# Two token tables instead of four, filled by long rows, and router logits with the router weights stationary in four column groups

## The chip, the cores and the metric

The kernel runs on one core of one Trainium2 chip. The metric is device time in microseconds (us) of one execution, the median of several runs. TensorE (PE) does matmuls, VectorE (DVE) and ScalarE (ACT) the elementwise work, GpSimd (POOL) small elementwise work and the indirect DMAs, and SyncE (SP) issues nearly all other DMAs, in program order.

## The reference, cut to what matters

```python
def _attn_ref(q, k, v, p):                      # batch 8, heads 8, seq 576, head_dim 64, 32 packed rows
    p_packed = sm_attn(p, k, v)
    return sm_attn(q, p_packed, p_packed)

def _moe_ref(x, w_in, w_out):                   # x: 4608 tokens x 512; d_ff 2048
    h = x @ w_in
    return (h * (1.0 / (1.0 + np.exp(-h)))) @ w_out

def _moe2_ref(x, w_gate, w_output_gate, w1, w2):    # 8 experts, F 1024
    logits = x @ w_gate
    e_idx = np.argmax(logits, axis=1)
    probs = softmax(logits)
    gate_w = probs[np.arange(N), e_idx]
    eom = 1.0 / (1.0 + np.exp(-(x @ w_output_gate)))
    for e in range(E):
        mask = e_idx == e
        h = np.maximum(x[mask] @ w1[e], 0.0)
        out[mask] = gate_w[mask, None] * eom[mask, e, None] * (h @ w2[e])
```

w_in and w_out arrive as 64-bit floats.

## The kernel before, in words

**Order.** The order of all instructions on each engine is written out by hand. Eight batches of 576 tokens go through attention and the dense layer. A batch is 16 steps, f = 0 to 15, one for each 128 columns of d_ff. A step (`batch`) runs: `mm1` (first matmul of column block f into the PSUM tile `h`, one buffer), `act` (tanh on ACT, L673, and the product `g` on DVE, L674, which reads `h`), the extra steps listed for position (f, 0), the splits of `g` into a rounded high part (`ghi`, ACT, L679) and a low part (`glo`, DVE, L684), in two of three steps of batches 1 to 6 a slot that splits a piece of expert weights (`shi` on ACT, L483, and a subtraction on DVE, L484), `mm2` for the column block two steps back, and the extra steps of position (f, 1). The next `mm1` needs the tile `h` to be free again. The extra steps at (f, 0) and (f, 1) are the attention of the next batch (s1 to s9: s3 is L579, s5 is L535 with the DVE transposes L603), `step_m` (L535 as ps_m), and the routing of the batch before.

**Batch 0.** It also converts w_in and w_out from 64 bits. `f64_load` brings a piece of 512 KB into one of six buffers, and `f64_conv` turns it into 32 bits by three DVE operations (L452, L455, L458), into `w_in` or into a tile `wf` (pool `stg`, two buffers) that ACT and POOL then split (L469, L470). Two pieces are converted in a step, and each conversion issues the load of the next piece. Value tiles of the next batch come by `load_att`: `v1` of batch 1 is issued at the end of step 5, when s3 of the first half has read the same buffer, and is read by s3 of the second half at the end of step 7.

**Token tables.** Four tables in DRAM (`perm`, 289 x 128 rows of 16 integers, 2.37 MB each) hold the tokens sorted by expert. At the end of step 4 of batch 0 `setup_late` fills them, one with 4608 and three with 0, from a tile of 289 integers per partition: L175, 16 rows of 1156 bytes per partition and table. The fill tiles are two `wf` buffers. Then a zero row of `xr` is written from a tile of its own. Later `place` computes where each token goes, and one indirect DMA for each block of 128 tokens (L782) writes it to table (block number) mod 4. Whoever reads a place (`fetch_ix`, L910) reads all four tables and adds the four (L911, L912).

**Router logits.** After the second matmul of a batch, `row_t` transposes a pair of token blocks (ACT and DVE copy them to SBUF), at steps 3 and 7 of the next batch, and `row_logits` multiplies them with the router weights at (5, 0) and (9, 0): for each of the two blocks 4 matmuls (L265) with the 128 x 128 block stationary and 8 router columns moving. DVE copies the 8 logits of each block out (L269), and when a group of blocks is complete `finish` (L738 to L741) finds the expert of each token. Groups of four blocks complete with the pair at step 9 (in batches 1, 3, 5, 7), groups of five with a single block at step 13 (batches 2, 4, 6). There are 16 pairs, 14 of them inside batches and 2 in `last_rows`, and 4 single blocks.

**Experts.** From about 870 us on, 38 blocks of sorted tokens are gathered and multiplied with their expert's weights.

Of the kernel before, what the change touches and what calls it, by code (L numbers as in the profile page):

```python
# [8 lines left out]
F32 = mybir.dt.float32  # L9
# [3 lines left out]
I32 = mybir.dt.int32  # L13
ALU = mybir.AluOpType
# [10 lines left out]
E8 = 8  # L25
F2 = 1024
NTOK = B * S
NBLK = NTOK // 128
CAP = NBLK
NPAIR = NBLK + E8 - 1  # L30
XW = DM + 1
SCALE = 1.0 / 8.0

C_ID, C_E, C_OFF, C_LT, C_J, C_END = 0, 128, 136, 144, 208, 209
HS = S // 2
EARLY = 3
NSTATIC = NBLK + 2
NPERM = 4
PW = 16


def constants():
    p = np.arange(128)
    c = np.zeros((128, C_END), np.float32)
    c[:, C_ID:C_ID + 128] = np.eye(128)
    e = np.arange(E8)
    c[:, C_E:C_E + E8] = e
    c[:, C_OFF:C_OFF + E8] = (e - E8) * CAP
    c[:, C_LT:C_LT + E8 * E8] = (e[None, :] < e[:, None]).reshape(1, -1)
    c[:, C_J] = p  # L50
    k = np.full((128, 256), 0x3F80, np.uint16)
    k[:, :128] *= p[:, None] < p[None, :]
    t = np.stack([block_tokens(i) for i in range(NBLK)], axis=1).astype(np.int32)
    t[:, np.arange(NBLK) % NPERM > 0] -= NTOK
    t = np.concatenate([t, np.zeros((128, PW - 1), np.int32)], axis=1)
    return {"cst": c, "cstk": k, "cstt": t}

# [24 lines left out]
class Kernel:  # L82
# [12 lines left out]
    def run(self):  # L95
        tc, nc = self.tc, self.nc
        c_const, cp = self.pool("const")
        c_rt, self.rt = self.pool("rt")
        c_p1, self.p1 = self.pool("p1")
        c_in, self.pin = self.pool("pin", "right")  # L100
        c_att, self.pa = self.pool("pa", "right")
        psums = [self.pool(n, space=PSUM) for n in ("ps_acc", "ps_h", "ps_a")]
        self.ps_acc, self.ps_h, self.ps_a = [p for _, p in psums]
        p1 = self.p1

        self.cst = cp.tile([128, C_END], F32, name="cst")
        self.ident = self.cst[:, C_ID:C_ID + 128]
        self.iota8 = self.cst[:, C_E:C_E + E8]
        self.tri = cp.tile([128, 2, 128], BF16, name="tri")
        self.nt_run = cp.tile([128, E8], F32, name="nt_run")  # L110
        self.pick_f = cp.tile([128, 40], F32, name="pick_f")
        self.before = cp.tile([128, E8, E8], F32, name="before")
        self.tb = cp.tile([128, 8, E8], F32, name="tb")
        self.pick_i = cp.tile([128, 8], U32, name="pick_i")
        self.ptab = cp.tile([1, 1 + EARLY], I32, name="ptab")
        self.tab = cp.tile([1, 4, NPAIR], I32, name="tab")

        self.flip = False
        self.ppt, self.m, self.g, self.loads = {}, {}, {}, {}
        self.graws = []  # L120
        self.wgt = cp.tile([128, 4, E8], F32, name="wgt")
        self.tok = self.rt.tile([128, NBLK + PW - 1], I32, name="tok")
        self.w_in = self.pin.tile([128, 4, FF], F32, name="w_in")
        self.a1 = [self.pa.tile([128, 5, 128], F32, name="a1t")]
        self.pp = self.pa.tile([128, 128], F32, name="pp")
        self.a2 = [[p1.tile([128, 2, S], F32R, tag=f"a2_0{i}", name="a2") for i in range(2)], None]
        self.zero = self.rt.tile([128, 512], BF16, tag="junk", bufs=1, name="zero")
        nc.gpsimd.memset(self.zero, 0.0)
        nc.gpsimd.memset(self.a1[0][64:128, 4, :], 0.0)

        self.split_jobs = [(w, e, k) for e in range(E8) for w in (1, 2) for k in range(4)]
        self.split_n, self.split_raw, self.split_loaded, self.split_done = 0, [], [], []
        self.late, self.group = [], None
        self.ch, self.ex, self.x, self.xt, self.hs, self.ht, self.sc = {}, {}, {}, {}, {}, {}, {}

        c_stg, self.stg = self.pool("stg", "right")
        self.wo = self.p2 = self.mid = None
        self.prologue()
        self.batch(0)
        c_stg.close()  # L140
        c_stg, self.stg = self.pool("spl", "right")
        for b in range(1, B - 1):
            self.batch(b)
        while self.split_jobs or self.split_loaded or self.split_done:
            self.split_store()
            self.split_slot()
        c_stg.close()
        c_att.close()
        self.pick()
        self.batch(B - 1, hook=lambda f: self.open_first(f, c_in))  # L150
        self.last_rows()
        c_p1.close()
        c_p2, self.p2 = self.pool("p2")
        c_q2, wp = self.pool("q2")
        self.r2 = tc.queue_regs(depth=2, engines=[ENG.SP, ENG.PE], name="r2")
        self.q2 = wp.queue([128, 4, 2, 2 * DM], F32R, regs=self.r2, name="q2", contiguous=True)
        self.experts()
        for c in (c_q2, c_p2, self.c_q1, *[c for c, _ in reversed(psums)], c_rt, c_const):
            c.close()
# [6 lines left out]
    def setup_late(self):  # L166
        nc = self.nc
        nc.sync.dma_start(self.tri, self.i["cstk"].bitcast(BF16).rearrange("p (a b) -> p a b", a=2))
        nc.sync.dma_start(self.tok, self.i["cstt"])
        nc.gpsimd.memset(self.nt_run, 0.0)  # L170
        for i, perm in enumerate(self.perm):
            if i < 2:
                fill = self.stg.tile([128, E8 * CAP + 1], I32, tag="wf", bufs=2, name="fill")
                nc.gpsimd.memset(fill, 0 if i else NTOK)
            nc.sync.dma_start(perm.rearrange("(p c) w -> p (c w)", p=128).rearrange("p (w c) -> p w c", w=PW),  # L175
                              fill.unsqueeze(1).to_broadcast([128, PW, E8 * CAP + 1]))
        z = self.rt.tile([128, 5, XW], F32, tag="xr", name="zrow")[:1, 0]
        nc.gpsimd.memset(z, 0.0)
        nc.sync.dma_start(self.xr[NTOK:NTOK + 1, :], z)

    def pick(self):
        assert self.group is None and not self.late
# [39 lines left out]
    def last_rows(self):  # L222
# [3 lines left out]
        g = self.rows_group(b, range(4))  # L226
        for j in (3, 0, 1, 2):
            self.mm2_block(self.acc[j], hi[:, j * 128:j * 128 + 128], lo[:, j * 128:j * 128 + 128], NF - 1, False, True)
        for j in (3, 0, 1, 2):
            self.evac(g, j, self.acc[j])  # L230
        acc = self.ps_acc.tile([128, 512], F32, tag="acc3", name="accL")
        side = {2: lambda: self.row_t(g, 3, 0), 5: lambda: self.row_logits(g, 3, 0),
                6: lambda: self.row_t(g, 1, 2), 9: lambda: self.row_logits(g, 1, 2),
                12: lambda: self.place(g)}
        for ff in range(NF):
            self.mm2_block(acc, self.gl[0][:, ff, :], self.gl[1][:, ff, :], ff, ff == 0, ff == NF - 1)
# [22 lines left out]
            g["t"][j] = t  # L259

    def row_logits(self, g, *js):
        ps = self.ps_a.tile([128, 2, 512], F32, tag="a", name="ps_rl")
        for n, j in enumerate(js):
            for k in range(4):
                self.nc.tensor.matmul(ps[:, 0, n * E8:n * E8 + E8], g["t"][j][:, k * 128:k * 128 + 128], self.wgt[:, k, :],  # L265
                                      start=(k == 0), stop=(k == 3))
        for n, j in enumerate(js):
            g["left"] -= 1
            self.nc.vector.tensor_copy(out=g["lg"][:, g["at"][j], :], in_=ps[:, 0, n * E8:n * E8 + E8])  # L269
        if not g["left"]:  # L270
            self.finish(g)

# [64 lines left out]
    def batch(self, b, hook=None):  # L337
        sched = self.extra_steps(b)
        for f in range(NF):
# [34 lines left out]
                    self.f64_load(t[:, i], True)  # L374
            if b == 0 and f == 14:
                self.mid = self.rt.tile([128, E8 * DM], F32, tag="wg", name="mid")
                self.nc.sync.dma_start(self.wgt, self.i["wgt"])
            if b == 0 and f == 15:
                self.split_load()
                self.split_load()  # L380
# [5 lines left out]
    def extra_steps(self, b):  # L386
        sched = {}

        def at(f, pos, fn):
            sched.setdefault((f, pos), []).append(fn)  # L390
# [13 lines left out]
        if b > 0:  # L404
            js = [(3, 0), (1, 2)] + ([(4,)] if b % 2 == 0 else [])
            for n, r in enumerate(js):
                at(4 * n + 3, 0, lambda r=r: self.row_t(self.group, *r))
                at(4 * n + 5, 0, lambda r=r: self.row_logits(self.group, *r))
            at(4 * len(js) + 3, 0, lambda: self.place(self.group))
        for c in range(1, 8):  # L410
            at(2 * c - 2 + (b == 0 and (c == 1 or c % 2 == 0)), 0, lambda c=c: self.step_m(b, c))
# [487 lines left out]
    def fetch_ix(self, j):  # L899
        nc = self.nc  # L900
# [3 lines left out]
        else:  # L904
            off = nc.values_load(self.tab[0:1, 0, j:j + 1], engines=[ENG.SP], min_val=0, max_val=E8 * CAP * 128)
            self.ex[j] = nc.values_load(self.tab[0:1, 1, j:j + 1], engines=[ENG.SP], min_val=0, max_val=E8 - 1)
        ix = self.rt.tile([128, NPERM + 2], I32, tag="xix_p", bufs=4, name="xix_p")
        at = self.rt.tile([128, 1], I32, tag="xix", bufs=6, name="xix")
        for i, perm in enumerate(self.perm):
            nc.sync.dma_start(ix[:, i:i + 1], perm[bass.ds(off, 128), 0:1])  # L910
        nc.gpsimd.tensor_tensor(out=ix[:, 4:6], in0=ix[:, 0:2], in1=ix[:, 2:4], op=ALU.add)  # L911
        nc.gpsimd.tensor_tensor(out=at, in0=ix[:, 4:5], in1=ix[:, 5:6], op=ALU.add)  # L912
        return at.bitcast(U32)

    def flag(self, j):
# [134 lines left out]
```

## Time and profile before

| what | value |
|---|---|
| median of 3 runs | 1361.1 us (1360.93 to 1362.29) |
| profiled execution | 1360.51 us, span 1358.7 us from first to last instruction |
| TensorE | busy 1269.3 us (93%), mean granted clock 0.971 |
| VectorE | 653.9 us (48%) |
| ScalarE | 505.8 us (37%) |
| GpSimd | 173.4 us (13%) |
| DMA | 247.72 MB, 182 GB/s on average |

Busy shares are averages over the whole span; the stages differ. A row of the timeline gives the start, the busy time, the engine and line, the operation, and in brackets how long the engine sat idle before it and what ended that.

### The profile page before, as it was taken

The numbers are of one execution on the slowest core, as the hardware profiler recorded it, in microseconds if no ns is written. First come the engines' busy times: TensorE is split into PE (matmuls) and PEld (weight loads), VectorE is DVE, ScalarE is ACT, GpSimd is POOL, SyncE is SP. The second block draws the span as 40 slices with busy tenths as digits, with TensorE's granted clock in tenths as the row PEclk, the third lists the DMA queues.
The fourth block names the chain that finished last, engine by engine and source line by source line (L and its number), as shares of the span: only waits on it lengthen the run. The fifth ranks groups of instructions, "written<-read, shape, count | busy, mean of one in ns | idle before, by whom it ended". The sixth has DMA issues, their size and how long they took to land. (4 is left out here: it accounts for less than half of the span.)

```text
span 1358.7 us, 24463 instructions
## 1 busy us (share of the span) xinstructions
PE 1269.3 (93%) x8414; PEld 1020.1 (75%) x8416; DVE 653.9 (48%) x1417; ACT 505.8 (37%) x980; POOL 173.4 (13%) x236
## 2 busy tenths in 40 slices
PE   7754699999999899999999999999999999999997
PEld 3543578778788688787787788878888888888886
DVE  6953965845865745857556745232222222222221
ACT  3321255445464444454454433223223222222322
POOL 0220310100010100101000111112212212211210
PEclk9686899999999999999999999999999999999999
DMA  7598346846695855776665414442557383722630
GB/s 292 205 233 210 110 151 222 274 158 223 211 292 180 257 197 189 227 285 209 225 219 193 104 32 157 108 127 71 193 173 249 121 301 97 277 66 69 236 129 23
DMA packets 118303, 247.72 MB, mean 182 GB/s; under 512 B 30177, under 2 KB 56609, under 8 KB 118178
## 3 DMA queue, kind: packets, MB, share of 16 engines
q1 hardware_dynamic: 110946, 226.35, 51.0%
q0 software_dynamic: 7232, 19.72, 4.4%
q8 instruction: 77, 1.26, 0.4%
q14 instruction: 48, 0.39, 0.1%
HBM read 401.92 MB, written 96.29 MB: 367 GB/s over the span
## 5 line engine op out<-in xcount | busy, mean ns | idle before, releaser
L715 PE MATMUL acc<-wo,ghi 128*128 128x512 f32 x1024 | 320.9, 395 | 0.0
L715 PEld LDWEIGHTS acc<-wo,ghi 128*128 128x128 f32 x1024 | 194.5, 190 | 39.0
L664 PE MATMUL ps_h<-a,m_hi 128*128 128x288 f32 x1024 | 215.5, 303 | 0.8 <-DVE a L630 0.8
L715 PE MATMUL acc<-wo,glo 128*128 128x512 f32 x512 | 212.9, 416 | 0.0
L664 PE MATMUL ps_h<-a,m_lo 128*128 128x288 f32 x512 | 163.5, 319 | 30.9 <-DVE g L674 25.2
L1007 PE MATMUL py<-queue_q_buf,hhi 128*128 x608 | 190.7, 395 | 0.0
L979 PE MATMUL pu<-queue_q_buf,xhi 128*128 x560 | 174.6, 393 | 0.0
L664 PEld LDWEIGHTS ps_h<-a,m_hi 128*128 128x128 f32 x1024 | 171.1, 196 | 2.7 <-DVE a L630 1.0
L993 DVE TENSOR_TENSOR hlo<-ph,hhi 128x512 fp32r<-128x512 f32 x76 | 49.0, 686 | 247.3 <-ACT hhi L992 247.3
L674 DVE SCALAR_TENSOR_TENSOR g<-g,ps_h 128x576 f32<-128x576 f32 x128 | 96.1, 751 | 131.0 <-ACT g L673 130.2
L673 ACT ACTIVATE g<-ps_h 128x576 f32<-128x576 f32 x128 | 83.3, 651 | 188.8 <-PE ps_h L664 186.0
L664 PEld LDWEIGHTS ps_h<-a,m_lo 128*128 128x128 f32 x512 | 99.8, 195 | 57.0 <-DVE g L674 33.3
L1007 PEld LDWEIGHTS py<-queue_q_buf,hhi 128*128 128x128 f32 x608 | 114.5, 188 | 25.6
L715 PEld LDWEIGHTS acc<-wo,glo 128*128 128x128 f32 x512 | 97.3, 190 | 43.0 <-issue 24.8
L1007 PE MATMUL py<-queue_q_buf,hlo 128*128 x304 | 122.9, 404 | 0.0
L979 PEld LDWEIGHTS pu<-queue_q_buf,xhi 128*128 128x128 f32 x560 | 105.3, 188 | 22.4
L782 POOL DMA_INDIRECT perm<-tok,dsti x36 | 38.9, 1081 | 647.9 <-DVE dsti L779 507.4
L679 ACT CAST ghi<-g 128x512 fp32r<-128x512 f32 x128 | 79.4, 620 | 107.6 <-DVE g L674 106.5
L979 PE MATMUL pu<-queue_q_buf,xlo 128*128 x280 | 113.7, 406 | 0.3 <-ACT hs L981 0.3
L981 ACT ACTIVATE hs<-pu 128x512 f32<-128x512 f32 x76 | 45.4, 598 | 164.2 <-PE pu L979 162.5
L684 DVE TENSOR_TENSOR glo<-g,ghi 128x512 fp32r<-128x512 f32 x128 | 88.5, 692 | 31.1 <-ACT ghi L679 26.2
L1012 POOL DMA_INDIRECT out<-y,xix x38 | 38.2, 1006 | 328.2 <-ACT y L1010 320.6
(183 smaller groups left out, 1501.1 us busy)
## 6 DMA issues: line engine op xcount, KB each, us to landing
queue_q_buf<-ws SPq DMA_DIRECT2D x70, 4096.0 KB
ws<-shi SPq DMA_DIRECT2D x64, 512.0 KB
mid<-in_w SPq DMA_DIRECT2D x48, 512.0 KB
ws<-mid SPq DMA_DIRECT2D x48, 512.0 KB
att_v<-in_v SPq DMA_DIRECT2D x15, 640.0 KB
perm<-fill SPq DMA_DIRECT2D x4, 2312.0 KB
og<-in_wog SPq DMA_DIRECT2D x35, 256.0 KB
att_k<-in_k SPq DMA_DIRECT2D x15, 576.0 KB
```

Of the source, the lines that this page charges most:

```text
L664: nc.tensor.matmul(ps[:, hf, :288], lw[:, qd, fs], rx[:, qd, ts], start=(i == 0), stop=(i == 5))
L673: nc.scalar.activation(out=g2, in_=ps[:, :, :288], func=AF.Tanh, scale=0.5)
L674: nc.vector.scalar_tensor_tensor(out=g2, in0=g2, scalar=1.0, in1=ps[:, :, :288], op0=ALU.add, op1=ALU.mult)
L679: self.nc.scalar.copy(out=hi, in_=self.graw[:, :512])
L684: self.nc.vector.tensor_tensor(out=lo, in0=self.graw[:, :512], in1=self.ghi.bitcast(F32), op=ALU.subtract)
L715: self.nc.tensor.matmul(acc, l, r, start=(first and i == 0), stop=(last and i == 2))
L782: nc.gpsimd.indirect_dma_start(out=self.perm[(i0 + r) % NPERM], out_offset=bass.IndirectOffsetOnAxis(ap=di[:, r:r + 1], axis=0), in_=self. ...
L979: nc.tensor.matmul(ps, l[:, ks], w[:, k, r, ns], start=(i == 0), stop=(i == 11))
L981: nc.scalar.activation(out=self.hs[j][:, n * 512:n * 512 + 512], in_=ps, func=AF.Relu)
L993: nc.vector.tensor_tensor(out=lo[:, n], in0=ps, in1=hi[:, n].bitcast(F32), op=ALU.subtract)
L1007: nc.tensor.matmul(ps, l[:, k // 4, ks], w[:, k // 2, r, (k % 2) * DM:(k % 2) * DM + DM], start=(i == 0), stop=(i == 23))
L1012: nc.gpsimd.indirect_dma_start(out=self.out, out_offset=bass.IndirectOffsetOnAxis(ap=ix[:, 0:1], axis=0), in_=y, in_offset=None, bounds_ch ...
```

## The change

The four tables become two. Both are filled with half of 4608 (and the token numbers are shifted by as much), from one tile of 2312 integers per partition, in two rows of 9248 bytes per partition and table; the tile lies in the `xr` buffer, not in the `wf` buffers. The zero row comes from a tile that is zero already. A place is read from two tables, with one addition. Blocks go to table (block number) mod 2.

For a pair of token blocks the logits now take 8 matmuls with 32 columns of router weights stationary (8 of the quarter meant, the rest of other quarters or zero) and 128 token columns moving, in four column groups of 32: two halves of the contraction for each of the two blocks. ACT copies the 128 x 128 result into SBUF, over the first 128 columns of the transposed second block, and after `mm2` of the same step, at (f, 1) and ahead of the attention's step there, one matmul with that copy stationary and a 0/1 selection of 16 columns moving adds the halves and turns the result back. It writes 16 columns of the tile `h` behind the columns that `act` has read. The copies of the logits and `finish` follow there. In `last_rows` the first part moves from block 5 to 4 and from 9 to 8, and the second takes its place. Single blocks stay as they were.

```diff
-C_ID, C_E, C_OFF, C_LT, C_J, C_END = 0, 128, 136, 144, 208, 209
+C_ID, C_E, C_OFF, C_LT, C_J, C_SEL, C_END = 0, 128, 136, 144, 208, 209, 225
-NPERM = 4
+NPERM = 2
...
+    n = np.arange(2 * E8)
+    c[:, C_SEL:] = (p[:, None] % 32 == n % E8) & (p[:, None] // 32 % 2 == n // E8)
...
-    t[:, np.arange(NBLK) % NPERM > 0] -= NTOK
+    t -= NTOK // NPERM
...
-        self.wgt = cp.tile([128, 4, E8], F32, name="wgt")
+        self.wgt = cp.tile([128, 3 * E8 + 32], F32, name="wgt")
...
-        for i, perm in enumerate(self.perm):
-            if i < 2:
-                fill = self.stg.tile([128, E8 * CAP + 1], I32, tag="wf", bufs=2, name="fill")
-                nc.gpsimd.memset(fill, 0 if i else NTOK)
-            nc.sync.dma_start(perm.rearrange("(p c) w -> p (c w)", p=128).rearrange("p (w c) -> p w c", w=PW),
-                              fill.unsqueeze(1).to_broadcast([128, PW, E8 * CAP + 1]))
-        z = self.rt.tile([128, 5, XW], F32, tag="xr", name="zrow")[:1, 0]
-        nc.gpsimd.memset(z, 0.0)
-        nc.sync.dma_start(self.xr[NTOK:NTOK + 1, :], z)
+        n = (E8 * CAP + 1) * PW // 2
+        fill = self.rt.tile([128, 5 * XW], I32, tag="xr", name="fill")[:, :n]
+        nc.gpsimd.memset(fill, NTOK // NPERM)
+        for perm in self.perm:
+            nc.sync.dma_start(perm.rearrange("(p c) w -> p (c w)", p=128).rearrange("p (h n) -> p h n", h=2),
+                              fill.unsqueeze(1).to_broadcast([128, 2, n]))
+        nc.sync.dma_start(self.xr[NTOK:NTOK + 1, :].rearrange("o (p c) -> (o p) c", p=3), self.zero.bitcast(F32)[:3, :XW // 3])
...
-        side = {2: lambda: self.row_t(g, 3, 0), 5: lambda: self.row_logits(g, 3, 0),
-                6: lambda: self.row_t(g, 1, 2), 9: lambda: self.row_logits(g, 1, 2),
+        side = {2: lambda: self.row_t(g, 3, 0), 4: lambda: self.row_logits(g, 3, 0), 5: lambda: self.row_logits2(g, (3, 0)),
+                6: lambda: self.row_t(g, 1, 2), 8: lambda: self.row_logits(g, 1, 2), 9: lambda: self.row_logits2(g, (1, 2)),
                 12: lambda: self.place(g)}
...
     def row_logits(self, g, *js):
+        nc = self.nc
         ps = self.ps_a.tile([128, 2, 512], F32, tag="a", name="ps_rl")
-        for n, j in enumerate(js):
+        if len(js) == 1:
             for k in range(4):
-                self.nc.tensor.matmul(ps[:, 0, n * E8:n * E8 + E8], g["t"][j][:, k * 128:k * 128 + 128], self.wgt[:, k, :],
-                                      start=(k == 0), stop=(k == 3))
+                nc.tensor.matmul(ps[:, 0, :E8], g["t"][js[0]][:, k * 128:k * 128 + 128], self.wgt[:, k * E8:k * E8 + E8], start=(k == 0), stop=(k == 3))
+            self.row_logits_out(g, ps[:, 0, :E8], js)
+            return
+        for k in (0, 2, 1, 3):
+            for n, j in enumerate(js):
+                c = 2 * (k // 2) + n
+                nc.tensor.matmul(ps[32 * c:32 * c + 32, 0, :128], self.wgt[:, k * E8:k * E8 + 32], g["t"][j][:, k * 128:k * 128 + 128],
+                                 start=(k % 2 == 0), stop=(k % 2 == 1))
+        g["part"] = g["t"][js[1]][:, :128]
+        nc.scalar.copy(out=g["part"], in_=ps[:, 0, :128])
+
+    def row_logits2(self, g, js, h=None):
+        ps = (self.ps_a.tile([128, 2, 512], F32, tag="a", name="ps_rl") if h is None else h)[:, 0, 288:288 + 2 * E8]
+        self.nc.tensor.matmul(ps, g["part"], self.cst[:, C_SEL:C_SEL + 2 * E8], start=True, stop=True)
+        self.row_logits_out(g, ps, js)
+
+    def row_logits_out(self, g, ps, js):
         for n, j in enumerate(js):
             g["left"] -= 1
-            self.nc.vector.tensor_copy(out=g["lg"][:, g["at"][j], :], in_=ps[:, 0, n * E8:n * E8 + E8])
+            self.nc.vector.tensor_copy(out=g["lg"][:, g["at"][j], :], in_=ps[:, n * E8:n * E8 + E8])
         if not g["left"]:
             self.finish(g)
...
-                self.nc.sync.dma_start(self.wgt, self.i["wgt"])
+                self.nc.vector.memset(self.wgt, 0.0)
+                self.nc.sync.dma_start(self.wgt[:, :4 * E8].rearrange("p (k e) -> p k e", e=E8), self.i["wgt"])
...
                 at(4 * n + 5, 0, lambda r=r: self.row_logits(self.group, *r))
+                if len(r) == 2:
+                    sched.setdefault((4 * n + 5, 1), []).insert(0, lambda r=r: self.row_logits2(self.group, r, self.h))
...
-        ix = self.rt.tile([128, NPERM + 2], I32, tag="xix_p", bufs=4, name="xix_p")
+        ix = self.rt.tile([128, NPERM], I32, tag="xix_p", bufs=4, name="xix_p")
...
-        nc.gpsimd.tensor_tensor(out=ix[:, 4:6], in0=ix[:, 0:2], in1=ix[:, 2:4], op=ALU.add)
-        nc.gpsimd.tensor_tensor(out=at, in0=ix[:, 4:5], in1=ix[:, 5:6], op=ALU.add)
+        nc.gpsimd.tensor_tensor(out=at, in0=ix[:, 0:1], in1=ix[:, 1:2], op=ALU.add)
```

## Rows read from the trace of the kernel before

**Rows 1.** The page: TensorE's busy tenths in 40 slices of 34 us.
```profile
PE   7754699999999899999999999999999999999997
```

**Rows 2.** Timeline of TensorE, 60 to 150 us, its two longest idle times.
```profile
85.69 0.61 PE L664 MATMUL ps_h<-a,m_lo 128*128 128x288 f32 x1 [11.54 <-DVE g L674]
...
121.63 1.30 PE L579 MATMUL ps_s<-att_v,a1t 128*32 128x64 f32 x40 [21.21 <-DMA att_v<-in_v]
```

**Rows 3.** Timeline of SyncE's queue, 60 to 130 us: start, time to issue.
```profile
68.99 23.88 SPq L175 DMA_DIRECT2D perm<-fill  x4
...
101.28 2.07 SPq L432 DMA_DIRECT2D stg<-in_w_out  x1
...
104.98 0.56 SPq L524 DMA_DIRECT2D att_v<-in_v  x1
```

**Rows 4.** Timeline of VectorE, 60 to 130 us.
```profile
83.09 0.43 DVE L452 TENSOR_SCALAR wf<-stg 128x512 uint32<-128x512 uint32 x1 [13.17 <-DMA perm<-fill]
...
96.70 0.42 DVE L452 TENSOR_SCALAR wf<-stg 128x512 uint32<-128x512 uint32 x1
...
102.78 0.69 DVE L458 SCALAR_TENSOR_TENSOR w_in<-stg,w_in 128x512 uint32<-128x512 uint32 x1
122.99 0.28 DVE L581 TENSOR_SCALAR pp<-ps_s,sm 128x64 f32<-128x64 f32 x1 [19.52 <-PE ps_s L579]
...
126.89 0.75 DVE L674 SCALAR_TENSOR_TENSOR g<-g,ps_h 128x576 f32<-128x576 f32 x1 [1.83 <-ACT g L673]
```

**Rows 5.** Windows: stretch, length, granted clock, DMA share, GB/s.
```profile
75.00:80.00 5.00, 0.86 1.10 229
...
120.00:125.00 5.00, 0.50 0.81 331
...
211.00:212.00 1.00, 1.00 1.02 410
```

**Rows 6.** Timeline of SyncE's queue, 180 to 240 us: a store, rows of 4096 bytes.
```profile
209.52 0.33 SPq L476 DMA_DIRECT2D ws<-sw  x1
```

**Rows 7.** Timeline of GpSimd, 60 to 110 us, the two fill tiles.
```profile
68.62 0.62 POOL L174 MEMSET fill<- 128x289 int32 x2
```

**Rows 8.** Timeline of all engines, step 5 of batch 2.
```profile
309.52 0.38 PE L664 MATMUL ps_h<-a,m_lo 128*128 128x288 f32 x1
...
311.19 1.85 PE L265 MATMUL ps_rl<-wgt,mid 128*128 128x8 f32 x16
...
312.87 0.62 ACT L679 CAST ghi<-g 128x512 fp32r<-128x512 f32 x1 [0.82 <-DVE g L674]
312.90 0.48 PE L715 MATMUL acc<-wo,glo 128*128 128x512 f32 x1
...
314.62 1.23 DVE L484 TENSOR_TENSOR mid<-mid,shi 128x1024 fp32r<-128x1024 f32 x1 [0.27 <-ACT shi L483]
...
315.84 0.77 PE L579 MATMUL ps_s<-att_v,a1t 128*32 128x64 f32 x40
316.54 0.40 PE L664 MATMUL ps_h<-a,m_lo 128*128 128x288 f32 x1
```

**Rows 9.** Timeline of VectorE, step 9 of batch 1.
```profile
235.07 0.24 DVE L269 COPY lg<-ps_rl 128x8 f32<-128x8 f32 x2 [0.19 <-PE ps_rl L265]
...
236.92 0.19 DVE L741 TENSOR_TENSOR oh<-cst,rt 128x32 bf16<-128x32 f32 x1
...
239.36 0.84 DVE L603 STREAM_TRANSPOSE x<-ps_s 128x288 f32<-128x288 f32 x2
```

**Rows 10.** Timeline of GpSimd, 740 to 905 us: a group of five blocks placed.
```profile
767.79 0.96 POOL L782 DMA_INDIRECT perm<-tok,dsti  x1 [121.73 <-DVE pick_f L184]
...
775.49 0.96 POOL L782 DMA_INDIRECT perm<-tok,dsti  x1 [2.94 <-DMA perm<-tok,dsti]
...
787.75 0.98 POOL L920 DMA_INDIRECT xs<-xr,xix  x1 [0.56 <-ACT g L673]
```

**Rows 11.** Timeline of all engines, 890 to 925 us: first transposes of a gathered block.
```profile
900.15 0.63 PE L948 MATMUL px<-cst,x 128*128 128x128 f32 x4 [1.18 <-DVE hlo L993]
```

## What is predicted, before the changed kernel was seen

> **What bounds the kernel now.** I read the page's slices first. TensorE is busy nine tenths or more of every slice from the fifth on [rows 1]; before that, in the first 136 us, it is not. So work taken off TensorE after batch 0 should come off the end, and in batch 0 the question is what TensorE waits for. Its timeline there has two long gaps [rows 2]: 11.54 us, ended by the product g of VectorE, and 21.21 us, ended by a load of value tiles (v1 of batch 1). Together that is 32.75 us, 2.4% of the span.
>
> The reader should see one cause behind both. SyncE issues the four table fills from 68.99 us, and its issue is held for 23.88 us [rows 3]; the next load of weights is issued at 101.28 us and v1 at 104.98 us. VectorE meanwhile stands 13.17 us before the conversion into wf, released by a fill [rows 4]: the fill's source lies in a wf buffer. That is the first gap, seen from VectorE. Then VectorE works on from 83.09 us through the six pieces that are still loaded, until 102.78 + 0.69 = 103.5 us, and stands 19.52 us more for s3 of TensorE [rows 4], which waits for v1. So the fills stop batch 0 twice: by the buffer, and by their place in front of v1 in the queue.
>
> How fast they run is in the windows: 229 GB/s at a DMA share of 1.10, all engines full, in rows of 1156 bytes [rows 5]. 4 x 2.37 = 9.47 MB at that rate are 41 us.
>
> **The fills, changed.** Bytes halve to 4.73 MB, in rows of 9248 bytes. The nearest long-row stores are those of split expert weights, 4096 bytes a row: the store issued at 209.52 us [rows 6] moves at 410 GB/s [rows 5]. The bounds are 229 GB/s (row length does nothing) and 410 GB/s. I take 400, nearest to the store rows: 11.8 us.
>
> The Trainium skill (DMA: Bandwidth & Descriptors, Specifications) puts line rate at 512 bytes and more, so by it 1156 and 9248 bytes would be alike. The trace does not agree so far, 229 against 410 GB/s, both stores from SBUF to DRAM; but the short rows also start at odd addresses, which the trace can't separate. By the rule the fill would take 20.7 us instead of 11.8; that is the first rival below.
>
> Now the steps. The memset grows from 2 x 289 to 2312 integers per partition: 0.62 us for 578 [rows 7] is 1.07 ns each, 2.5 us. So the fills are issued at 68.6 + 2.5 = 71.1 us rather than 69.0. VectorE may then start the conversion at 71.1 (its own work is done at 83.09 - 13.17 = 69.9; I let it wait for the memset, which costs about 1 us and may be nothing). Against 83.09 that is 12.0 us earlier. The wf buffers are free, so steps 5 to 7 run as before, and VectorE is ready for v1's s3 result at 103.5 - 12.0 = 91.5 us; TensorE is ready for s3 at 121.63 - 21.21 - 12.0 = 88.4 us.
>
> When does v1 land? Issue to data takes some 1.4 us (the store of 209.52 us is still moving at 212 us: 0.52 MB at 410 GB/s is 1.3 us, so it began near 210.9). Fill: 71.1 + 1.4 + 11.8 = 84.3 us. Behind it, as before, two weight pieces and v1, 0.52 + 0.52 + 0.66 = 1.70 MB, 4.3 us, and 1.3 us to completion: 89.9 us. TensorE waits 1.5 us instead of 21.21, s3 takes some 0.8 us, and VectorE at 91.5 us waits for nothing. So this point moves from 122.99 to 91.5 us: a gain of 31.5 us. One thing more: after the long gap TensorE ran at a granted clock of 0.50, the lower of its two levels (1.2 of 2.4 GHz) [rows 5], its next matmuls took longer, and VectorE waited 1.83 us for them through ACT [rows 4]; after a gap of 1.5 us I expect no such drop. Sum 33.3 us. The rest of batch 0 was set by VectorE and by TensorE and moves along.
>
> At 229 GB/s the fill takes 20.7 us and ends at 93.2, v1 lands at 98.8 and VectorE goes on at 100.2 with the slow clock: the gain is 22.8 us. If VectorE doesn't wait for the memset, about 1 us more than my sum.
>
> **Logits, first part.** Before, the pair takes 312.90 - 311.19 = 1.71 us of TensorE [rows 8]. The nearest row for four column groups is s3, 20 matmuls of 64 columns, five deep in each group, 0.77 us with the way into and out of that mode [rows 8]; ours are 8 matmuls of 128 columns, two deep, 256 columns for a group where s3 has 320. Bounds 0.62 (in proportion) and 0.77; I take 0.68. The second matmul, two passes with 128 x 128 stationary: two of the 16 records that made 1.85 us [rows 8], 0.22 us. So 0.81 us less for a pair, 13.0 us for 16. The ACT copy in between falls where ACT waits for g anyway: 0.82 us of idle time before ghi [rows 8]. Without that cover it would cost 0.3 us for a pair, off TensorE's path by two steps.
>
> The Trainium skill (TensorEngine Tiling (Array Packing), Key Properties) says that changing the tiling mode drains TensorE, which speaks against the change; s3's row has both changes inside its 0.77 us, so by row and rule the sum is the same unless that row hides part of a drain.
>
> **Logits, the new wait.** The second matmul writes into tile h, and the next mm1 needs that tile free: it now waits for VectorE's two copies of the logits, and ahead of these on VectorE stands the slot's subtraction L484. In step 5 of batch 2 that ends at 314.62 + 1.23 = 315.85; two copies, 0.24 us [rows 9], and some 0.2 us of signalling put mm1 at 316.3. Before it started at 316.54 [rows 8]. Without the wait it would start at 311.19 + 0.68 + 2.94 (mm2) + 0.22 + 0.70 (s3) = 315.73. So where a slot stands in the step, 0.25 us are left of 0.81. Two of three steps have one; of the 14 pairs 8 do (step 5 of batches 2, 3, 5, 6; step 9 of batches 1, 2, 4, 5). In step 9 of batches 1, 3 and 5 finish comes along as well: behind the copies it takes from 235.07 + 0.24 to 236.92 + 0.19, 1.8 us [rows 9]. It lay under mm2 and now stands ahead of the transposes L603, 0.84 us, for which step_m waits. That is 2.6 us of VectorE against 1.67 us of mm1 (309.52 to 311.19, [rows 8]): step_m waits 1.0 us more. Batch 7 has no attention step behind which the copies hide: they cost 0.24 us and two signals, 0.7 us, and 0.1 us is left of each of its pairs. Where no slot stands, 0.8 us stay. Sum: three such pairs (batches 1 and 4 at step 5, 6 at step 9) 2.4; six with a slot alone 1.5; batches 1 and 5 at step 9 (slot and finish) lose 0.75 each; batch 3 there (finish alone: 0.84 + 1.8 us of VectorE behind the copies, less s5's cover) 0.1; batch 7 0.2; the two pairs of last_rows, where no h is in play, 1.6. That is 4.3 us of 13.0.
>
> **Two tables.** A third block of a group now waits for the first to land. In the group of five the fifth waits so already, 775.49 - 767.79 = 7.7 us after the first [rows 10]. Now the last block of five goes out about 15.4 us after the first, 8 us later than before. GpSimd has nothing else due: the gather behind it is issued at step 4 of batch 7 and first used at step 13, nine steps of up to 7 us (309.52 to 316.54, [rows 8]) later. I cost that at nothing; without this cover it is 8 us once. The last blocks, ahead of the expert stage's first reads, are the place where the cover is thinnest: nothing to 8 us, and I take nothing, since these reads have to wait for the table of experts first. Each read of a place loses two DMAs and one addition, which TensorE covers through the expert stage [rows 1], but for the first gathered block, before which TensorE idles 1.18 us [rows 11]. The row names VectorE's hlo, which the second matmul after it needs too, so I take 0.5 us of gain; nothing and 1.2 us are the bounds. The memset and load of wgt, the longer cst and the zero row lie in queues that have no late reader: nothing.
>
> **Sum.** 33.3 + 4.3 + 0.5 = 38.1 us. The profiled execution took 1360.5 us, 0.6 below the median of the runs: 1322.4 there, 1323 us as a median.
>
> **The rivals.**
> First, the rate stays at 229 GB/s: the fills gain 22.8 and the clock is lost, 1361.1 - 22.8 - 4.8 = 1333.5 us. For it: only loads and stores of 4096 aligned bytes are seen to be fast. Against it: the same stores' 410 GB/s.
> Second, the wait on h costs nothing because the copies get through earlier than I think: 13.0 instead of 4.3, 1314 us. For it: my 0.2 us of signalling; against it: L484 ends after mm2.
> Third, the wait costs more: VectorE is late by up to 1.5 us in each of 14 steps, 21 lost against 13 gained, 1335 us.
> Fourth, slower than before: the column groups don't run beside each other and weight loads are not hidden. Then a pair's first part takes 4 x 0.68 us and 16 weight loads of 0.11 us, the pair 4.7 us, 3.0 more than 1.71: 48 lost in 16 pairs against 33.8 gained, 1375 us. It decides from 2.1 us more for a pair on. Against it: s3's row itself, where 40 records share 0.77 us.
>
> **How the numbers follow.** Forecast 0.52 (1319 to 1327 by itself), first rival 0.13, second 0.15, third 0.15, fourth 0.03, anything else 0.02. The range from 1313 to 1337 takes in all but the fourth and the far ends. A change under 0.2%, 2.7 us, can hardly be told from none here. Faster by more 0.96, within 0.01, slower 0.03.
>
> **What would show it.** In the changed profile: fills at 380 GB/s or more over 12 us; no wait of VectorE on a fill; TensorE's wait for v1 under 4 us; pp near 91 us; a pair's first part at 0.6 to 0.8 us; and new waits of mm1 on the logits' copies, 0.5 us each, where a slot stands in the step. It goes wrong if v1 lands after 95 us, if another load is late next, or if mm1's new waits come to more than 1 us.

## The result, and the profile after

The changed kernel takes 1325.03 us (median of 4 runs, 1324.27 to 1326.56) against 1361.01 us: ratio 0.9736, 95% interval 0.9719 to 0.9753. The forecast was 1323, with a range of 1313 to 1337. The profiled execution took 1325.14 us, span 1323.4 us against 1358.7; TensorE was busy 1254.0 us (95%) at a mean granted clock of 0.986 (before 0.971).

The page's slices of TensorE in the changed kernel:

```profile
PE   6687999999998999999999999999999999999997
```

Against [rows 1] the third, fourth and fifth slices rise from 5, 4 and 6 tenths to 8, 7 and 9; from the sixth slice on the two look alike, so the large gain must lie in batch 0. There the queue of SyncE shows (start, time to issue):

```profile
72.63 1.29 SPq L177 DMA_DIRECT2D perm<-fill  x2
73.97 1.31 SPq L179 DMA_DIRECT2D xr<-zero  x1
75.38 0.91 SPq L451 DMA_DIRECT2D stg<-in_w_out  x1
...
80.02 1.21 SPq L543 DMA_DIRECT2D att_v<-in_v  x1
```

In the kernel before, the write of the zero row stood between the fills and the next weight load as well:

```profile
92.97 8.21 SPq L179 DMA_DIRECT2D xr<-zrow  x1
```

The fills hold the queue 1.29 us instead of 23.88, and the zero row behind them 1.31 instead of 8.21; the next weight load goes out at 75.38 instead of 101.28 and v1 at 80.02 instead of 104.98 [rows 3]. The windows say how fast the fill runs (stretch, length, granted clock, DMA share, GB/s):

```profile
75.00:80.00 5.00, 1.00 1.03 425
...
90.00:95.00 5.00, 1.00 0.95 362
```

425 GB/s where the short rows had 229 [rows 5]; 4.73 MB at that rate are 11.1 us. The DMA packets in the trace say how long it took: the fills' run from 73.92 to 87.18 us, 13.3 us. The clock is at 1.00, its upper level, in these stretches, where before it fell to 0.50 behind the long gap. Later in batch 0 it falls once more, behind a wait of 3.37 us that ends at 111.04 us (the kernel before has the like, 3.27 us, at 142.69):

```profile
115.00:120.00 5.00, 0.50 0.00 0
```

At 91.90 us TensorE waits 1.82 us for v1, in its timeline

```profile
91.90 0.77 PE L598 MATMUL ps_s<-att_v,a1t 128*32 128x64 f32 x40 [1.82 <-DMA att_v<-in_v]
```

and VectorE never stands before a fill. Its timeline:

```profile
69.36 3.27 DVE L588 TENSOR_SCALAR sm<-sm 128x2 f32<-128x2 f32 x1
...
72.74 0.42 DVE L471 TENSOR_SCALAR wf<-stg 128x512 uint32<-128x512 uint32 x1
...
93.07 0.28 DVE L600 TENSOR_SCALAR pp<-ps_s,sm 128x64 f32<-128x64 f32 x1
...
95.23 0.76 DVE L693 SCALAR_TENSOR_TENSOR g<-g,ps_h 128x576 f32<-128x576 f32 x1
```

The timeline of GpSimd there:

```profile
70.57 2.03 POOL L175 MEMSET fill<- 128x2312 int32 x1
```

The conversion into wf starts at 72.74 instead of 83.09, pp at 93.07 instead of 122.99, g at 95.23 instead of 126.89 [rows 4]. (This execution began its first g 1.91 us later than the one before, so in the clock of before these are 1.9 us earlier.)

The logits are seen in step 5 of batch 2, the timeline of all engines, 32.06 us earlier than [rows 8]:

```profile
279.22 0.64 PE L272 MATMUL ps_rl<-mid,wgt 128*32 128x128 f32 x16
...
279.79 0.50 PE L734 MATMUL acc<-wo,glo 128*128 128x512 f32 x1
...
282.54 1.23 DVE L503 TENSOR_TENSOR mid<-mid,shi 128x1024 fp32r<-128x1024 f32 x1 [0.27 <-ACT shi L502]
282.65 0.29 PE L279 MATMUL ps_h<-cst,mid 128*128 128x16 f32 x2
...
282.87 0.77 PE L598 MATMUL ps_s<-att_v,a1t 128*32 128x64 f32 x40
...
283.69 0.23 DVE L285 COPY lg<-ps_h 128x8 f32<-128x8 f32 x2
...
284.06 0.37 PE L683 MATMUL ps_h<-a,m_lo 128*128 128x288 f32 x1 [0.43 <-DVE lg L285]
```

First part 0.57 us (279.22 to 279.79), second 0.22 (282.65 to 282.87), together 0.79 instead of 1.71. Then the new wait: s3 is done, and mm1 stands 0.43 us until VectorE has copied the logits, which it can't do before the slot's subtraction of 282.54. Over all batches the table of TensorE's waits (us, times, longest) from 130 to 830 us has

```profile
PE ps_h L683 <- DVE lg L285: 3.2, 7, 0.5
PE ps_m L554 <- DVE x L622: 2.0, 3, 0.7
PE ps_h L683 <- DVE mx L757: 1.5, 3, 0.5
```

All three are new: mm1 for the copies, step_m for the transposes behind finish, mm1 for finish's own reading.

The next table divides the span by marks in the timelines: the first g of VectorE in batch 0; from g of step 4 to g of step 8 of batch 0; from the first g of batch 1 to the last of batch 7; from there to the seventh `hs` of ACT in the expert stage; from that to the 76th and last `hs`. It holds all kernels of this study.

| kernel | to first g | batch 0, steps 4 to 8 | batches 1 to 7 | tail | experts |
|---|---|---|---|---|---|
| before | 31.99 | 63.42 | 662.72 | 63.70 | 430.58 |
| after | 33.90 | 29.83 | 657.33 | 62.36 | 433.29 |
| e1 fills only | 31.56 | 32.30 | 662.70 | 63.31 | 431.38 |
| e2 logits only | 32.11 | 61.58 | 657.35 | 63.18 | 433.28 |
| e3 short rows | 31.96 | 42.03 | 657.25 | 62.25 | 433.12 |
| e4 wider constants only | 31.51 | 60.75 | 662.48 | 63.77 | 433.28 |
| e5 buffer only | 30.96 | 60.62 | 664.37 | 63.82 | 430.58 |
| e6 ACT copies | 31.68 | 29.85 | 655.24 | 62.50 | 433.27 |
| e7 ACT copies, late finish, padded | 32.10 | 29.74 | 655.42 | 62.98 | 430.58 |
| e8 four tables, long rows | 32.19 | 42.60 | 659.72 | 65.06 | 433.29 |
| e9 place behind mm2 | 32.51 | 29.75 | 664.82 | 63.04 | 430.58 |
| e10 padded only | 32.26 | 30.27 | 657.23 | 63.53 | 431.42 |
| e11 place first | 30.91 | 30.70 | 656.43 | 62.39 | 431.47 |

After against before: 33.6 us gained in steps 4 to 8 of batch 0, 5.4 in batches 1 to 7, 1.3 in the tail; 0.1 lost in the rest of batch 0, 1.9 in the prologue of this execution, 2.7 in the expert stage and 0.3 behind the last `hs`. That is the 35.3 us between the spans. The loss in the expert stage was in nobody's sum.

Each row of the table is one execution, and they come from several chips. In steps 4 to 8 the four kernels that fill four tables by short rows take 60.62 to 63.42 us, the seven with the fills as changed 29.74 to 32.30. So the 33.6 us of this pair are known to some 3 us only.

### The profile page after: what moved, and what is told of

Its sections match the earlier page's. It is cut to its first block, busy times and chain, and to the rows that moved or that the text cites. A ratio compares the mean times of both kernels' runs of the same rounds, so it can differ in the third digit from the quotient of the medians.

```text
span 1323.4 us, 24265 instructions
## 1 busy us (share of the span) xinstructions
PE 1254.0 (95%) x8446; PEld 999.3 (76%) x8448; DVE 654.4 (49%) x1418; ACT 508.5 (38%) x996; POOL 166.5 (13%) x196
## 5 line engine op out<-in xcount | busy, mean ns | idle before, releaser
L683 PE MATMUL ps_h<-a,m_hi 128*128 128x288 f32 x1024 | 210.6, 298 | 0.8 <-DVE a L649 0.8
L683 PE MATMUL ps_h<-a,m_lo 128*128 128x288 f32 x512 | 160.5, 313 | 22.9 <-DVE g L693 15.6
L683 PEld LDWEIGHTS ps_h<-a,m_hi 128*128 128x128 f32 x1024 | 166.8, 191 | 2.7 <-DVE a L649 1.0
```

The costliest lines, as they stand in the source:

```text
L683: nc.tensor.matmul(ps[:, hf, :288], lw[:, qd, fs], rx[:, qd, ts], start=(i == 0), stop=(i == 5))
```

## The experiments

Each ratio is against the kernel before on the same chip, with its 95% interval.

**The two halves of the change, each alone.** e1 has the fills, tables, zero row and fetch of the change and the logits, with the widths of their constants, of before; e2 has the logits of the change and the four tables of before. The edits, in words:

```diff
 e1: as changed, but
-            at (5, 0): first part; at (5, 1): second part into tile h
+            at (5, 0): 8 matmuls for each pair as before, DVE copies behind them
 e2: as changed, but
-NPERM = 2 and one fill tile in the xr buffer
+NPERM = 4 and two fill tiles in wf buffers, 16 rows of 1156 bytes
```

> The tables' part alone (two tables, long rows, the other fill buffer), logits as before. Theory: batch 0 is all of it, 33.6 us between steps 4 and 8, so 1327.4 us if the two losses seen in the changed kernel (prologue 1.9 us later, 2.7 us lost over the expert stage) come with the logits part's wider constants, and 1332 us if they come with the tables. Rival (the tables give little and the logits the most): 1345 us or more.

> The logits' part alone, tables and fills as before. Theory: the pairs save 0.8 us each and lose most of it to mm1's wait on the logits' copies; 5.4 us in the batches and 1.3 in last_rows, so 1354.3 us, or 1359 us if the two small losses come with the wider constants. Rival (no wait on h): 13 us, 1348 us. Both gaps of batch 0, 11.5 and 21.2 us, stay.

e1: 1327.98 against 1358.72 us, 0.9778 (0.9763 to 0.9793), 30.7 us less. e2: 1354.72, 0.9974 (0.9965 to 0.9984), 4.0 less. Together 34.7; the whole change gave 36.0 in its own comparison. So within the intervals the parts add up, and neither hides the other. The table of stages puts each where it belongs: e1 has batches 1 to 7 as before (662.70), e2 batch 0 nearly as before (61.58) and batches 1 to 7 as changed (657.35).

**Rows, bytes and the buffer.** What in the fills gains? e3 writes the two tables by 16 short rows; e8 writes four tables by four rows of 4624 bytes, so bytes as before and rows long; e5 changes nothing but the place of the fill tiles (and the zero row's source).

```diff
 e3: as changed, but
-  perm.rearrange("p (h n) -> p h n", h=2),  fill.unsqueeze(1).to_broadcast([128, 2, n])
+  perm.rearrange("p (h n) -> p h n", h=16), fill[:, :n // 8].unsqueeze(1).to_broadcast([128, 16, n // 8])
 e8: as changed, but NPERM = 4, two fill tiles of 1156 integers in the xr buffer, and
+  perm.rearrange("p (h n) -> p h n", h=4),  both[:, min(i, 1)].unsqueeze(1).to_broadcast([128, 4, n])
 e5: as before, but
-                fill = self.stg.tile([128, E8 * CAP + 1], I32, tag="wf", bufs=2, name="fill")
+                fill = both[:, i]            # both: two tiles of 289 integers in the xr buffer
...
```

> The changed kernel with its two fills written in 16 rows of 1156 bytes per partition instead of 2 of 9248, the same bytes. Theory (row length sets the rate, 229 against some 410 GB/s): the fill takes about 9 us more, v1 lands about 9 us later, 1333 to 1335 us. Rival (line rate from 512 bytes on, only the halved bytes count): 1325 us.

> The changed kernel with four tables again, each filled in 4 rows of 4624 bytes per partition from two tiles of half the length: twice the bytes, long rows. Theory (400 GB/s): 9.47 MB take 23.7 us, v1 lands about 12 us later than in the changed kernel, 1336 us, near the two tables with short rows. Rival (bytes count, rows don't): the fills take 41 us and nearly all of the 33 us come back, 1352 to 1355 us.

> The kernel before, its four fills in rows of 1156 bytes as they were, but their source in the xr buffer, so that no conversion waits for a wf buffer. Theory (the place in the queue ahead of v1 sets the end of the stall): the gap of 11.5 us goes and comes back in front of v1, 1359 to 1361 us on a chip where the kernel before takes 1361. Rival (the buffer is half of the stall): 12 us less, 1349 us.

e3: 1336.32 against 1358.72, 0.9848 (0.9832 to 0.9864). e8: 1340.22 against 1359.88, 0.9855 (0.984 to 0.987). e5: 1359.51 against 1359.88, 0.9998 (0.9989 to 1.0008): no change.

The windows of e3:

```profile
75.00:80.00 5.00, 1.00 1.10 227
...
85.00:90.00 5.00, 1.00 1.13 193
90.00:95.00 5.00, 0.54 1.12 187
```

The windows of e8:

```profile
75.00:80.00 5.00, 1.00 1.02 401
80.00:85.00 5.00, 1.00 1.01 409
85.00:90.00 5.00, 1.00 1.02 412
```

The DMA share is above 1 in both: the engines are full either way, but with short rows they move half as much. Now the table of TensorE's waits from 60 to 130 us, the longest one, first in e3:

```profile
PE ps_s L598 <- DMA att_v<-in_v: 12.5, 1, 12.5
```

in e8:

```profile
PE ps_s L599 <- DMA att_v<-in_v: 13.2, 1, 13.2
```

and in e5:

```profile
PE ps_s L579 <- DMA att_v<-in_v: 32.1, 1, 32.1
```

In e5 the gap of 11.54 us [rows 2] is gone, and the wait for v1 has grown from 21.21 to 32.1, by 10.9: freeing the buffer alone moves the stall to the next thing that is late, the queue. There the zero row, written as in the change, still holds the queue 8.24 us behind the fills, so that hold too comes from the fills ahead of it. The other half alone, a fast fill out of the old wf buffers, wasn't built: whether the change needs the free buffer isn't shown. In e3 and e8, which each keep one of the two savings, v1 is 12.5 and 13.2 us late instead of 1.8. Steps 4 to 8 take 42.03 and 42.60 us where before takes 63.42 and the change 29.83: either saving with the free buffer is worth some 21 us, and the second the last 12 to 13. e8 is also 2.4 us longer than the change in batches 1 to 7 and 2.7 in the tail; why wasn't followed up. e3 is the first rival of the prediction, built: 22.4 us less than before, where the rival had 27.6. Of the 5.2 us between them the table shows 2.5 in the expert stage and 1.4 in steps 4 to 8, where the rival had 22.8 us of gain and e3 has 21.4; the rest isn't placed. The 1.4 go with a rate that falls below 200 GB/s at the end of the fill, which it does in the kernel before as well, in its windows:

```profile
95.00:100.00 5.00, 1.00 1.11 227
105.00:110.00 5.00, 0.50 1.10 181
```

Why the end of the fill is slower stays open.

**The new wait.** e6 lets ACT copy the pair's logits instead of VectorE, so that they don't queue behind the slot's subtraction.

```diff
-            self.nc.vector.tensor_copy(out=g["lg"][:, g["at"][j], :], in_=ps[:, n * E8:n * E8 + E8])
+            if len(js) == 2:
+                self.nc.scalar.copy(out=g["lg"][:, g["at"][j], :], in_=ps[:, n * E8:n * E8 + E8])
...
```

> The changed kernel with the two copies of a pair's logits on ScalarE instead of VectorE, which frees tile h before the slot's subtraction ends. Theory: 0.4 to 0.5 us in each of the 8 pair steps with a slot, 3 to 4 us less than the changed kernel, its times of 1325 becoming 1321. Rival (something else holds mm1 there): no change.

1322.36 against 1359.88, 0.9729 (0.9715 to 0.9744): its interval overlaps that of the change, so the time alone doesn't tell. The trace does: batches 1 to 7 take 655.24 us instead of 657.33, and mm1's waits for the logits (3.2 and, for finish, 1.5 us) are down to one row,

```profile
PE ps_h L686 <- ACT lg L286: 0.6, 2, 0.3
```

The wait was real. These rows fall by 4.1 us in all, but batches 1 to 7 by only 2.1, where 3 to 4 were expected: about 2 us is what the wait cost.

**The expert stage.** The change adds 16 columns to the constants and 24 to the router weights in SBUF. e4 is the kernel before with only these widths.

```diff
-C_ID, C_E, C_OFF, C_LT, C_J, C_END = 0, 128, 136, 144, 208, 209
+C_ID, C_E, C_OFF, C_LT, C_J, C_SEL, C_END = 0, 128, 136, 144, 208, 209, 225
...
-        self.wgt = cp.tile([128, 4, E8], F32, name="wgt")
+        self.wgt = cp.tile([128, 7, E8], F32, name="wgt")[:, :4]
```

> The kernel before with only the wider constants: 225 instead of 209 columns loaded at the start, and 56 columns instead of 32 held for the router weights; nothing else. If the later start of batch 0 (1.9 us) and the slower expert stage (2.7 us) of the changed kernel come from these, 1365.6 us; from the later start alone 1363; if neither, 1361 us.

1360.54 against 1358.72, 1.0019 (1.001 to 1.0028): 1.8 us slower, with nothing computed differently. The groups by line of TensorE in 350 us of the expert stage (busy, mean ns of one, idle), in the kernel before:

```profile
L979 PE MATMUL pu<-queue_q_buf,xhi 128*128 x443 | 138.2, 393 | 0.0
...
L979 PE MATMUL pu<-queue_q_buf,xlo 128*128 x222 | 90.2, 406 | 0.0
```

The same groups in the changed kernel:

```profile
L997 PE MATMUL pu<-queue_q_buf,xhi 128*128 x440 | 138.7, 396 | 0.0
...
L997 PE MATMUL pu<-queue_q_buf,xlo 128*128 x220 | 90.0, 409 | 0.0
```

And in e4:

```profile
L979 PE MATMUL pu<-queue_q_buf,xhi 128*128 x440 | 138.7, 396 | 0.0
L979 PE MATMUL pu<-queue_q_buf,xlo 128*128 x220 | 90.0, 409 | 0.0
```

Each of the 840 first matmuls of the experts (560 and 280) is 3 ns longer in the mean: 2.5 of the 2.7 us. The second matmuls take the same (395 and 394 ns). All six kernels with the wider constants, unpadded, need 433.1 to 433.3 us for the stage. e10 pads the router weights of the changed kernel by 24 columns more, and nothing else.

```diff
-        self.wgt = cp.tile([128, 3 * E8 + 32], F32, name="wgt")
+        self.wgt = cp.tile([128, 3 * E8 + 32 + 24], F32, name="wgt")[:, :3 * E8 + 32]
```

> The changed kernel with nothing but 24 unused columns behind the router weights, so that the tiles behind the constants lie 256 instead of 160 bytes further than in the kernel before. Theory (the lay of the tiles makes the expert stage slower): the expert stage takes as long as in the kernel before, 2.6 us less than in the changed kernel, which is 0.2% of its time. Rival (ScalarE copies or the put-off finish did that): no change.

1322.76 against 1357.94, 0.9738 (0.9724 to 0.9751): no gain that the time shows over the change's 0.9736. In the trace the stage takes 431.42 us, 1.9 less; two other kernels padded alike (e7, e9) take 430.58 as before, a third (e11) 431.47. And e1, whose constants are as narrow as before, takes 431.38. So 24 columns more take most of the loss back again: it is not the width as such. That it is the place of the tiles behind the constants fits all the runs, but which tile and which address isn't shown, nor what makes the last 0.8 to 0.9 us.

**Better versions.** e7 takes e6, the padding, and puts finish of a pair off to the kernel's list of late work, behind the transposes that step_m waits for. e9 also moves `place` of the groups of four from before to after mm2, at the end of the list there; e11 puts it at the front of that list.

```diff
 e7: as e6, padded as e10, and
+        if not g["left"] and len(js) == 2:
+            self.late.append(lambda: self.finish(g))
 e9: as e7, and
-            at(4 * len(js) + 3, 0, lambda: self.place(self.group))
+            at(4 * len(js) + 3, int(len(js) == 2), lambda: self.place(self.group))
 e11: as e7, and, for len(js) == 2
+            sched.setdefault((11, 1), []).insert(0, lambda: self.place(self.group))
```

> As the one with ScalarE copies, and finish put off to the next step's list of late work, and the router weights' tile padded so that everything behind the constants lies 256 instead of 160 bytes further than in the kernel before. Theory: step_m no longer waits for the transposes in step 10 of batches 1, 3 and 5, 1 us each; if the lay of the tiles made the expert stage 2.7 us slower, a shift of 256 bytes may undo it: 1315 to 1318 us with both, 1318 to 1320 with the first alone. Rival (any shift costs): the expert stage stays 2.7 us slower.

> ScalarE copies, finish put off, the padded constants, and place moved behind mm2 of its step in the batches that close a group of four. Theory: the 1.3 us that TensorE waited in place for the put-off finish goes, 1 us in each of batches 1, 3 and 5: 3 us less than the same kernel without the move, 1316 to 1317 us where the kernel before takes 1361. Rival (place's later result makes the next group's work late): no gain.

> As the one that moved place behind mm2, but place stands ahead of the attention's step there, so that VectorE reads its result before it waits for ScalarE in that step. Theory (step_m of step 12 waited for the buffer of place, held by VectorE's place in line): the 10 us lost there go, and the 1.3 us of each early place as well, 0.967 to 0.968 of the kernel before. Rival (place behind mm2 is late whatever its order): 0.975 or more.

e7: 1319.36 against 1359.88, 0.9709 (0.9695 to 0.9723); e9: 1329.24 against 1357.94, 0.9795 (0.9781 to 0.9808); e11: 1320.8 against 1358.82, 0.9725 (0.9712 to 0.9738). The table of TensorE's waits from 130 to 830 us, its rows for the routing, in e7:

```profile
PE ps_r L788 <- DVE oh L765: 4.7, 3, 1.6
```

in e9:

```profile
PE ps_m L559 <- DVE nt_run L794: 9.9, 3, 3.9
```

and in e11, with the wait of mm1 for g:

```profile
PE ps_h L691 <- DVE g L701: 14.5, 13, 2.2
PE ps_m L562 <- DVE nt_run L797: 3.3, 2, 1.7
```

In e7 the expert stage gained what was expected, batches 1 to 7 did not: the late finish removes step_m's wait and gives TensorE another of 4.7 us in place, whose matmul needs finish's result: batches 1 to 7 stay at 655.4. Moving place doesn't remove that wait either. In e9 step_m of the next step waits until VectorE has read place's PSUM tile, and VectorE does so only behind the attention's work; 9 us are lost, where 3 were to be gained. In e11, the wait on g is up from 9.3 us in e7 to 14.5, and step_m's wait is 3.3: the 4.7 us are paid in other rows, and batches 1 to 7 are 1.0 us longer than in e7, 0.7 of it in the last steps of batch 5. I expected e11 to beat e7; it missed. Of the kernels here e7 has the lowest ratio. It is measured faster than e6 on the same chip by 3.0 us, of which the expert stage shows 2.7 in the trace; the two intervals overlap a little.

## Why the prediction was right, step by step

- **The page's slices.** I read TensorE as busy nine tenths from the fifth slice on. The fifth slice is at 6 [rows 1]; nine tenths begin with the sixth, at 170 us and not at 136. The fifth lies in batch 0 as well, so nothing in the sum hangs on it.
- **The fills** (33.3 us): 33.6. One cause behind both gaps, as read: with the fill tiles elsewhere and the queue free both went. v1 was to be read at 89.9 us; TensorE went on at 91.90, which less the late start of 1.9 us is 90.0. The wait was 1.82 us where 1.5 was forecast, pp came at 93.07 - 1.9 = 91.2 where 91.5 was, and the clock was not low behind v1. That it fits to 0.1 us is partly luck. The fills took 13.3 us rather than 11.8, although they ran at 425 GB/s for a stretch; and the 1.3 us to completion, for which no row stood, were 0.6: the last packet of v1 ends at 91.30 us. The gain itself is known to some 3 us; e1, the fills alone, has 31.1 in its profile.
- **Row length.** The Trainium skill (DMA: Bandwidth & Descriptors, Specifications) has line rate from 512 bytes on. Here it does not hold: 1156-byte rows ran at 227 GB/s in e3, 4624-byte rows at 401 to 412 in e8, 9248-byte rows at 425; from the first packet of the fill to the last that is 198, 369 and 357 GB/s in the mean. The rows of e8 start at multiples of 16 bytes, not of 4096, so alignment to 4096 is not what makes rows fast; rows of 1156 bytes that start at round addresses weren't tried.
- **VectorE beside the memset.** I let VectorE wait for the memset, at about 1 us. It does: the two-column operation that should take 0.17 us (its time at 277.48 in batch 2) lasts 3.27 and ends at 72.63 us, with the memset (70.57 + 2.03 = 72.60). But it began at 69.36, before the memset, while GpSimd was at work on wo, and in the kernel before it stood 2.30 us at the same place and ended with GpSimd's last memset (69.17 + 0.52 = 69.69). So what the longer memset added is 0.97 us. First the changed kernel's rows, then those of before:

```profile
69.07 1.52 POOL L489 TENSOR_TENSOR wo<-wf,wo 128x512 fp32r<-128x512 f32 x1 [1.36 <-ACT wo L488]
```

```profile
67.42 2.30 DVE L569 TENSOR_SCALAR sm<-sm 128x2 f32<-128x2 f32 x1
...
69.17 0.52 POOL L178 MEMSET zrow<- 1x513 f32 x1
```

- **First and second part** (0.68 and 0.22 us): 0.57 and 0.22. Four groups do run beside each other, and the price came below both bounds, 0.62 to 0.77. The fourth rival is excluded.
- **The wait on h** (2.7 us left in the batches): 5.4. The step was right, the size too small by half. In step 5 of batch 2 the subtraction ended, in the clock of before, at 283.77 + 32.06 = 315.83, forecast 315.85; but the copies began at its heels and mm1 followed 0.14 us after them, at 316.12 instead of 316.3. The second rival, a free wait, had 8.7 us more in the batches and last_rows together; e6, which takes the wait nearly away, gained 2.1. The third, a dearer wait, would have lost time in every pair; only two did. Counted from one g to the next, pairs with a slot alone kept 0.44 to 0.48 us at step 5 and 0.33 at step 9 instead of 0.25, by the shorter signals, since there the end of the subtraction sets mm1. Pairs without a slot kept 0.88 to 0.95 instead of 0.8, by the cheaper first part. At step 9 with slot and finish, batch 1 lost 0.54 and batch 5 lost 0.17, where 0.75 each was forecast. Of the 2.7 us more than forecast, the six pairs with a slot alone make 1.1 and these two 0.8.
- **last_rows** (1.6 us): the tail gained 1.3, but that is no clean measure of it. e2, with the logits alone, gained 0.5 there and e1, with the logits of before, 0.4; whether the two pairs gave what was forecast isn't shown. There the first part takes 820.34 to 820.91 = 0.57 us and the second 0.14, in the timeline of TensorE

```profile
820.34 0.65 PE L272 MATMUL ps_rl<-xrt,wgt 128*32 128x128 f32 x16
820.91 0.96 PE L734 MATMUL accL<-wo,gl 128*128 128x512 f32 x3
821.72 0.29 PE L279 MATMUL ps_rl<-cst,xrt 128*128 128x16 f32 x2
821.86 0.94 PE L734 MATMUL accL<-wo,gl 128*128 128x512 f32 x3
```

- **Fetch** (0.5 us): 0.1. TensorE idles 1.10 us before the first gathered block where it was 1.18 [rows 11], still for VectorE's hlo: the reads of places weren't late. The term was taken between two bounds, with no row that said where.

```profile
861.77 0.63 PE L966 MATMUL px<-cst,x 128*128 128x128 f32 x4 [1.10 <-DVE hlo L1011]
```

- **Two tables** (nothing): the third block of a group does wait for the first now, 3.75 us in this row of GpSimd's timeline, and no row of TensorE shows a wait that came of it; batches 1 to 7 take as long with four tables (e2, 657.35) as with two (657.33). In the group of five the last block went out 8.9 us after the first (731.29 to 740.19 us), where 15.4 was forecast and 7.7 stood before.

```profile
798.50 0.96 POOL L801 DMA_INDIRECT perm<-tok,dsti  x1 [3.75 <-DMA perm<-tok,dsti]
```

- **Not in the sum:** "the longer cst" and the wider wgt, costed at nothing because nobody reads them late, cost 2.7 us in the expert stage (e4). The late start of 1.9 us is in one execution; the twelve other profiles, with and without the wider constants, begin at 30.9 to 32.5, so I don't put it down to the change. Without it the profiled execution would have taken 1323.2 us; as the other runs agree with the profiled one within 1.5 us, whether they start late too isn't shown.

That the total came within about 2 us is luck in part: the batches' 2.7 us too few and the experts' 2.7 us too many cancel. The large term was right by itself, as closely as these profiles can tell.

## What to carry to other kernels

When a bulk DMA stalls a stage, look for everything it delays, the buffer that it reads from and the queue in front of the next load: here freeing the buffer alone moved the stall to the queue and gained nothing (e5). Write constants by few long rows out of a tile that nobody else needs. Before taking a matmul's result into another tile that the next step wants, ask what already stands in the queue of the engine that must read it.

## What the runs showed of the hardware that was not expected

- Four column groups of 32 with 128 columns moving: 8 matmuls in 0.57 us, where the same products as 8 columns moving took 1.71.
- A fill in 1156-byte rows slowed from 227 GB/s to 181 in a late stretch of the kernel before and to 193 in e3.
- Behind fills in such rows the write of one 2 KB row held SyncE's queue 8.21 us, and 1.31 us behind the long ones.
- A VectorE operation on two columns, 0.17 us elsewhere, lasted 3.27 us beside GpSimd's work on wo and its memset, and ended with the memset.
- Matmuls of one stage took 396 ns in the mean instead of 393 when nothing but the width of constants was changed that they don't read (e4).
